# Attention and gated MLP on one core: a planned, pinned instruction order, fp32r transposes and column halves

## The chip, the core and the metric

The kernel runs on one core of a Trainium2 chip. The time is device microseconds of one execution; three runs of the kernel before gave a median of 826.99 us (826.61 to 827.62). A core has five instruction queues: TensorE (PE; its weight loads are shown apart as PEld), VectorE (DVE), ScalarE (ACT), GpSimd (POOL) and SyncE (SP), which here issues all DMA copies. Each queue is worked off in its order; an instruction that waits holds up those behind it.

## The reference

Attention over 8 batches of 8 heads, 576 tokens, head width 64, and then a gated MLP over each batch.

```
scores = q @ k.T / 8                       # per head, 576 x 576
cum    = cumsum(max(s, 0))                 # per head
scores = where(causal, -1e9, scores + min(-(cum[:, None] - cum[None, :]), 0))
attn   = softmax(scores)
x      = concat_heads(attn @ v)            # 576 x 512 per batch
h      = gelu_tanh(x @ w_in)               # 512 -> 1024
u, v   = h[:, :512], h[:, 512:]
v_n    = (v - mean(v)) / sqrt(var(v) + 1e-6) * g_ln
v_s    = w_sg @ v_n + b_sg[:, None]        # 576 x 576 over the tokens
out    = x + (u * v_s) @ w_out             # 512 -> 512
```

All inputs and the output are fp32 (the two weight matrices come as bits of 64-bit floats and are narrowed in the kernel).

## The kernel before

**Precision.** TensorE's fast type for 4-byte numbers here is fp32r. A product in fp32 quality is made of three fp32r products: each operand is split into a high part (a cast) and a low part (source minus high part), and high x high, high x low and low x high are added up in PSUM. `split` (L86) makes the two parts with one instruction on one engine and one on another. The first `NQ` = 8 heads do their scores, and the first `NP` = 12 heads their value products, in plain fp32 instead (tiles kf, qf, vf), which takes two instructions for each product and no splits.

**A head.** `load` (L102) fetches k, q and v; `split_head` (L272) splits them and copies rows into the combined operands by five DMA copies (L281 to L285). `scores` (L341) forms the causal 576 x 576 scores in five row blocks, of 448, 64, 320, 192 and 576 columns (the last in two halves), in two PSUM banks (ps_sc). `ttr` (L300) adds the mask and takes the row minimum on DVE (L305), `exp_` (L311) does the exponential with its row sum on ACT (L315), `norm` (L318) divides by the row sums on POOL (L338; ACT for one block of the fp32 heads). `transposes` (L365) turns the 13 blocks of 128 x 128 probabilities on TensorE (L377, in fp32, against an identity) into two banks (ps_pt) in four groups of 4, 4, 2 and 3; each group is evacuated by `evac` (ACT casts the high part, DVE subtracts the low one). `pv` (L432) multiplies them with v into the single bank xx (L450, L463 to L472), and ACT and DVE (L478, L479) add the upper and the lower 64 rows into the result tile xr, of which there are 8, four to a batch.

**A batch's MLP.** `ffn` (L484) splits xr into four xs tiles (POOL) and then does units of 12 to 14 matmuls: five v units (L518; the fifth, of 64 tokens, needs the last rows of xs side by side, which four DMA copies to xq bring, L528), eight u units (L582), eight s units (L597, L600, L601, the token mixing; L600 and L601 read the fifth v unit's result vnr), and eight o units (L616). Three banks (ps_m) serve these, in the last batch all but xx. After the v units DVE, ACT and POOL do the layer norm, and after each u unit the GELU.

**Order.** The text of the program is laid out on a time axis counted in heads: `place` puts steps at times (`POS`, L55), `spread` gives the units of a batch's MLP the stretch from 8b + 10 on, so that it lies beside the heads of the next batch. The framework's own scheduler (`schedule_with_timeline_sim=True`, L719) then moves instructions by its model of their durations. Weight blocks are fetched and split in the first 14 heads (`part`, L202); their DMA copies stand in `with later()` (L99), which puts them behind head 0's copy of cf (the cumulative sums) into k.

Of the kernel before, what the change touches and what calls it, by code (L numbers as in the profile page):

```python
# [40 lines left out]
         "o00 o01 s10 s11 s12 s13 o03 o02 o11 o13 o10 o12")  # L41
ORD0 = ("v0 v1 v2 v3 v4 u00 u01 u02 u10 u11 s00 u12 u03 s01 s03 u13 s02 o00 o01 s10 s11 s12 s13 o03 o02 o11 o13 o10 o12")
ORDL = ("v0 u00 v1 v2 u01 u02 v3 v4 u10 u11 s00 u12 u03 s01 s03 u13 s10 "
        "s02 o00 o01 s11 s12 s13 o03 o02 o11 o13 o10 o12")
CV = 1.4
# [5 lines left out]
MT = 52.0  # L51
F6 = [2.0, 9.4]
F7 = [2.0, 9.4]
F0 = [1.9, 9.6]
POS = dict(load=-1.8, split=-0.18, sc=(0, 0, 0, 0), tr=(0, 0, 0, 0), pv=(0, 0.1, 0.1), wv=(0.1, 6.0),  # L55
           wu=(7.0, 10.0), ws=(9.0, 11.0), wo=(11.0, 14.0), f0=2.0, f1=9.6)
# [3 lines left out]
def tile_attn_gmlp(  # L60
# [12 lines left out]
    nc = tc.nc  # L73

    const = ctx.enter_context(tc.tile_pool(name="const", bufs=1))
    att = ctx.enter_context(tc.tile_pool(name="att", bufs=2))
    moe = ctx.enter_context(tc.tile_pool(name="moe", bufs=1))
    ps_sc = ctx.enter_context(tc.tile_pool(name="ps_sc", bufs=2, space=bass.MemoryType.PSUM))
    ps_pt = ctx.enter_context(tc.tile_pool(name="ps_pt", bufs=2, space=bass.MemoryType.PSUM))
    ps_x = ctx.enter_context(tc.tile_pool(name="ps_x", bufs=1, space=bass.MemoryType.PSUM))  # L80
    ps_m = ctx.enter_context(tc.tile_pool(name="ps_m", bufs=3, space=bass.MemoryType.PSUM))
# [15 lines left out]
    first = []  # L97

    def later():  # L99
        return tc.issue_after(first[0].ins)  # L100

    def load(h):  # L102
        d = heads[h] = {}
        if h < NQ:
# [4 lines left out]
            x = nc.sync.dma_start(out=k[D:D + 1, :], in_=cf[h:h + 1, :])  # L109
            if h == 0:  # L110
                first.append(x)
        else:
            d["raw"] = att.tile([P, S], F32, name="raw", tag="raw", bufs=1)
            with later():
                nc.sync.dma_start(out=d["raw"], in_=kq[h, 0:2 * D])
# [3 lines left out]
        else:  # L119
            d["vr"] = att.tile([P, 6, D], F32, name="vr", tag="vr", bufs=1)  # L120
            with later():
                nc.sync.dma_start(out=d["vr"], in_=vp[h])

# [27 lines left out]
    load(0)  # L151
# [5 lines left out]
    ident = const.tile([P, P], F32, name="ident")  # L157
    nc.vector.memset(ident, 0.0)
# [14 lines left out]


    q2 = []
    pbuf = []
    sums = []
    for i in range(2):
        t = const.tile([66, S], F32R, name=f"q2_{i}")
# [3 lines left out]
        for it in range(5):  # L183
            t = const.tile([P, PW[it]], F32, name=f"p_{i}_{it}")
            if PW[it] > ITW[it]:
                nc.gpsimd.memset(t[:, ITW[it]:PW[it]], 0.0)
# [538 lines left out]
```

## Time and profile before

| | |
|---|---|
| median of three runs | 826.99 us |
| the profiled execution, its span | 828.8 us |
| PE busy | 792.6 us, 96% |
| DVE, ACT, POOL busy | 597.9, 576.5, 595.1 us, 70 to 72% |
| DMA | 89.29 MB, mean 108 GB/s |
| TensorE's clock, mean | 0.991 |

The span runs from the first instruction's start to the last one's end. Busy time is the union of an engine's instructions; matmuls overlap in a pipeline, so a matmul's duration in the trace is longer than the distance to the next one, and a busy TensorE may still be stalled. "Idle before, releaser" at the end of a row tells how long the engine did nothing before it, and what ended that. The chain of waits follows the last instruction back to what released it, step by step.

### The profile page before, as it was taken

Reading aid. Unit: us, or ns where it says so; the run is one execution under the profiler, and the core shown is the slowest. Engines: PE = TensorE matmul, PEld = TensorE weight load, DVE = VectorE, ACT = ScalarE, POOL = GpSimd, SP = SyncE. Lnnn points to the kernel's source line nnn. Section 1 sums busy time; section 2 is a strip of 40 time slices with the busy share of each in tenths; the row PEclk is TensorE's granted clock in tenths of the full one; section 3 lists DMA queues with packets and bytes.
Section 4 is the critical chain, followed back from the end, with each engine's and each line's share of the span. In section 5 each row is a group of like instructions: output and inputs, shape, how many; then the busy total and the mean of one; then the engine's idle time right before and its main releaser. Section 6 shows DMA issues by size and latency. Waiting matters only on the chain.

```text
span 828.8 us, 16733 instructions
## 1 busy us (share of the span) xinstructions
PE 792.6 (96%) x5161; PEld 696.1 (84%) x5161; DVE 597.9 (72%) x1806; ACT 576.5 (70%) x1620; POOL 595.1 (72%) x979
## 2 busy tenths in 40 slices
PE   6899999899999999999989999999999999999878
PEld 3355666889989998999979998899989998899778
DVE  5995468975787578966888577965888678963652
ACT  4787778775686678866878577866787677862430
POOL 4987668878677768796768778785778778872451
PEclk9999999999999999999999999999999999999989
DMA  7656553343442543444434453443444353400101
GB/s 210 215 158 181 148 139 84 86 105 100 116 106 74 128 125 86 108 121 126 112 82 104 115 139 90 113 109 96 119 119 103 100 152 93 98 26 23 35 8 57
DMA packets 69804, 89.29 MB, mean 108 GB/s; under 512 B 25954, under 2 KB 42212, under 8 KB 69716
## 3 DMA queue, kind: packets, MB, share of 16 engines
q1 hardware_dynamic: 69716, 88.23, 40.8%
q8 instruction: 41, 0.67, 0.4%
q14 instruction: 47, 0.39, 0.2%
HBM read 42.27 MB, written 9.73 MB: 63 GB/s over the span
## 4 chain that ended last, share of the span: by engine, by line
PE 73%; DVE 12%; DMA 5%; ACT 3%; issue 3%; POOL 2%; SPq 1%; DVEq 0%; POOLq 0%; ACTq 0%
PE om L616 12%; PE sm L597 11%; PE um L582 10%; PE xx L450 10%; PE vm L518 9%; PE pt L377 8%; PE sc L297 4%; PE sc L298 4%; DVE p L305 2%; DMA xq<-xs 2%; DMA q<-k 2%; PE sm L601 1%; PE sm L600 1%; DVE wbits L220 1%; DVE vm L504 1%
## 5 line engine op out<-in xcount | busy, mean ns | idle before, releaser
L338 POOL TENSOR_SCALAR p<-p,rs 128x448 f32<-128x448 f32 (+4 forms) x372 | 180.5, 499 | 29.1 <-DVE rs L321 9.6
L315 ACT ACTIVATE p<-p,mn 128x448 f32<-128x448 f32 (+4 forms) x320 | 177.9, 557 | 24.5 <-DVE mn L305 22.4
L305 DVE CUSTOM_DVE_ANT_0 p<-sc,mask 64x64 f32<-64x64 f32 (+4 forms) x320 | 126.2, 422 | 56.4 <-PE pt L377 31.0
L377 PE MATMUL pt<-ident,p 128*128 128x128 f32 (+1 forms) x832 | 137.2, 278 | 5.3 <-DVE pbl L389 2.6
L597 PE MATMUL sm<-ws,vn 128*128 128x288 f32 x768 | 130.3, 304 | 0.7 <-POOL vn L567 0.6
L93 POOL TENSOR_TENSOR k<-raw,k 128x576 fp32r<-128x576 f32 x56 | 80.3, 1433 | 66.7 <-ACT k L88 33.3
L582 PE MATMUL um<-xs,wi 128*128 128x288 f32 x768 | 123.4, 300 | 2.5 <-DVE u L504 2.4
L616 PE MATMUL om<-gt,wo 128*128 128x288 f32 x768 | 125.7, 298 | 0.0
L582 PEld LDWEIGHTS um<-xs,wi 128*128 128x128 f32 x768 | 108.9, 188 | 8.9 <-DVE u L504 4.0
L597 PEld LDWEIGHTS sm<-ws,vn 128*128 128x128 f32 x768 | 112.4, 192 | 3.3 <-DVE u L504 1.0
L377 PEld LDWEIGHTS pt<-ident,p 128*128 128x128 f32 (+1 forms) x832 | 96.8, 138 | 21.8 <-DVE pbl L389 5.4
L616 PEld LDWEIGHTS om<-gt,wo 128*128 128x128 f32 x768 | 110.6, 188 | 2.3
L518 PE MATMUL vm<-wi,xs 128*128 128x512 f32 x384 | 103.4, 399 | 0.0
L297 PE MATMUL sc<-k,q 128*128 128x448 f32 x336 | 100.8, 308 | 1.5 <-DVE mn L305 0.8
L298 PE MATMUL sc<-k,q 66*128 66x448 f32 x336 | 89.3, 298 | 0.6 <-DMA k<-cum 0.6
L88 ACT CAST pbh<-pt 128x512 fp32r<-128x512 f32 x104 | 48.9, 479 | 58.8 <-PE pt L377 58.8
L518 PEld LDWEIGHTS vm<-wi,xs 128*128 128x128 f32 x384 | 69.7, 189 | 14.9 <-POOL xs L93 1.6
L93 POOL TENSOR_TENSOR gt<-u,gt 128x288 fp32r<-128x288 f32 x64 | 50.7, 806 | 41.6 <-ACT gt L88 41.1
L297 PEld LDWEIGHTS sc<-k,q 128*128 128x128 f32 x336 | 60.8, 181 | 9.1 <-DVE mn L305 3.9
L93 DVE TENSOR_TENSOR pbl<-pt,pbh 128x512 fp32r<-128x512 f32 x104 | 56.5, 549 | 15.9 <-ACT pbh L88 15.9
L298 PEld LDWEIGHTS sc<-k,q 66*128 66x128 f32 x336 | 60.9, 181 | 5.9 <-issue 0.9
L88 ACT CAST k<-raw 128x576 fp32r<-128x576 f32 x56 | 37.6, 671 | 39.5 <-PE sc L297 33.8
(142 smaller groups left out, 1704.8 us busy)
## 6 DMA issues: line engine op xcount, KB each, us to landing
q<-k SPq DMA_DIRECT2D x168, 144.0 KB
raw<-in_kq SPq DMA_DIRECT2D x56, 288.0 KB
vr<-in_vp SPq DMA_DIRECT2D x52, 192.0 KB
out_t<-ot SPq DMA_DIRECT2D x64, 144.0 KB
k<-k SPq DMA_DIRECT2D x56, 144.0 KB
wraw<-in_w_in SPq DMA_DIRECT2D x16, 256.0 KB
kf<-in_kq SPq DMA_DIRECT2D x8, 288.0 KB
qf<-in_kq SPq DMA_DIRECT2D x8, 288.0 KB
```

Of the source, the lines that this page charges most:

```text
L88: nc.scalar.copy(out=hi, in_=src)
L93: eng_lo.tensor_tensor(out=lo, in0=src, in1=hi.bitcast(F32), op=ALU.subtract)
L297: nc.tensor.matmul(o, d["q1"][:, i0:i0 + r], d["k1"][:, j0:j1], start=True, stop=False)
L298: nc.tensor.matmul(o, q2[h % 2][:, i0:i0 + r], d["k2"][0:66, j0:j1], start=False, stop=True)
L305: nc.vector.tensor_tensor_reduce(out=pbuf[h % 2][it][0:r, j0:j1], in0=pst[0:r, c0:c0 + j1 - j0], in1=(mask2 if it in (2, 4) else mask)[0:r ...
L315: nc.scalar.activation(out=p, in_=p, func=AF.Exp, bias=d["mn"][0:r, it:it + 1], scale=-1.0, accum_out=sums[h % 2][0:r, it:it + 1])
L338: e.tensor_scalar(out=po, in0=pi, scalar1=f, scalar2=1.0, op0=ALU.mult, op1=ALU.mult)
L377: nc.tensor.transpose(out=ps[0:n, c:c + P], in_=pb[it][:, jb:jb + n], identity=ident)
L518: nc.tensor.matmul(ps[0:r], xs[c][:, xi, ts_], wi[:, c, wj, fs], start=(n == 0), stop=(n == 11))
L582: nc.tensor.matmul(ps[:, 0:CH], wi[:, c, wj, dt * P:(dt + 1) * P], xs[c][:, xi, cs], start=(n == 0), stop=(n == 11))
L597: nc.tensor.matmul(ps[:, 0:CH], vn[j][:, vi, ds_], ws[:, j, wj, cs], start=(n == 0), stop=False)
L616: nc.tensor.matmul(ps[:, 0:CH], wo[:, c, wj, ms], gt[ch, c][:, gi, :], start=(n == 0), stop=(n == 11))
```

## The change

1. **A planner writes the order.** Every engine call is recorded as an `Op` with its dependencies (by tile slot and region) and a cost (`cost`). `Plan.order` walks through them as a list scheduler: for each engine the earliest-written operation that is ready is taken; an operation becomes ready when its inputs' ends plus a latency for its engine (`LAT`, 454 ns for PE) have passed. Matmuls in a `group()` stay together; others may be interleaved one by one. The program is then issued in this order and not moved again (`manual_schedule`). SBUF slots are laid out by hand (`Ring`), and a slot can be held until `drop`. In its profile every engine instruction bears line 211, that of `issue`; its tiles tell them apart.
2. **Transposes in fp32r**: the probabilities are read through a second name of the same memory (`rbuf`) and the identity and the output are fp32r.
3. **14 result tiles** xr instead of 8; the xs splits are placed apart from the MLP units, earlier on the axis (`xsplit`).
4. **Column halves in fp32 heads**: the value products alternate between rows 0 to 63 and 64 to 127 of the xx bank; a third ACT copy and a DVE addition bring both together.
5. The `later()` around weight copies is gone; a head's k and v loads and splits are placed separately; four o units move ahead of three s units in each batch.

The counts of instructions are the same on TensorE, POOL and SP; DVE and ACT have 12 more each.

```diff
-ORDER = ("v0 u00 v1 u01 v2 u02 v3 v4 u10 u11 s00 u12 u03 s01 s03 u13 s02 "
-         "o00 o01 s10 s11 s12 s13 o03 o02 o11 o13 o10 o12")
+ORDER = ("v0 u00 v1 u01 v2 u02 v3 v4 u10 u11 s00 u12 u03 s01 s03 u13 s02 "
+         "o00 o01 s10 o03 o02 s11 s12 s13 o11 o13 o10 o12")
...
-POS = dict(load=-1.8, split=-0.18, sc=(0, 0, 0, 0), tr=(0, 0, 0, 0), pv=(0, 0.1, 0.1), wv=(0.1, 6.0),
-           wu=(7.0, 10.0), ws=(9.0, 11.0), wo=(11.0, 14.0), f0=2.0, f1=9.6)
+POS = dict(lk=-1.9, lkf=-1.55, lv=-1.35, lvf=-0.45, sk=-1.1, sv=-0.4, sc=(0, 0.15, 0.3, 0.4), cx=(1.0, 1.1, 1.2, 1.25, 1.35, 1.4, 1.45, 1.5), wv=(0.1, 6.0), wu=(5.0, 9.0),
+           ws=(8.5, 11.0), wo=(10.5, 13.0), f0=10.0, x0=2.4)
+LAT = dict(PE=454.0, ACT=136.0, DVE=136.0, POOL=185.0, SP=160.0)
+XR = 14
...
+    def order(self, lat=LAT):
...
+        while True:
+            best = None
+            for e, r in ready.items():
+                if r:
+                    t = max(free[e], min(r)[0])
+                    if best is None or t < best[0]:
+                        best = t, e
+            if best is None:
+                break
+            t, e = best
+            r = ready[e]
+            k = min(k for x, k in r if x <= t)
+            r.remove((rt[k], k))
+            o = ops[k]
...
+            for u in o.users:
+                q = ops[u]
+                q.left -= 1
+                if q.eng == e and e != "SP" and k not in q.raw:
+                    x = free[e]
+                else:
+                    x = end[k] + lat[q.eng]
+                rt[u] = max(rt[u], x)
+                if not q.left:
+                    push(u)
...
+    def issue(self, order):
+        for k in order:
+            for fn, args, kw in self.ops[k].calls:
+                fn(*args, **kw)
...
+    pbuf = [[pools[f"p{it}"]([P, PW[it]], F32, "p", i) for it in range(5)] for i in range(2)]
+    rbuf = [[pools[f"p{it}"]([P, PW[it]], F32R, "r", i) for it in range(5)] for i in range(2)]
...
-            nc.tensor.transpose(out=ps[0:n, c:c + P], in_=pb[it][:, jb:jb + n], identity=ident)
+            nc.tensor.transpose(out=ps[0:n, o:o + P].bitcast(F32R), in_=pb[it][:, jb:jb + n], identity=ident)
...
+        def mm(o0, o1, jt, m, side=0, k=P, **kw):
+            o = xx[D * side:D * side + rows, o0:o1]
+            nc.tensor.matmul(o, st(jt)[0:k], m, **{"start": False, "stop": False, **kw})
...
+        if f32:
+            with nc.group():
+                mm(64, 512, 1, pb_[0][:, 320:768], side=1, start=True)
+                mm(0, 512, 0, pa[0], start=True)
...
         if f32:
...
+            with nc.group():
+                mm(128, 448, 2, pb_[0][:, 0:320], side=1)
+                mm(192, 384, 3, pd[0][:, 128:320])
+                mm(0, 64, 0, pd[0][:, 64:128], side=1, stop=True)
+                mm(256, 320, 4, pd[0][0:REM, 0:64], k=REM, stop=True)
+            with nc.group():
+                nc.scalar.copy(out=xt[hs, 0:64], in_=xx[64:128, 0:64])
+                nc.scalar.copy(out=xt[hs, 64:128], in_=xx[0:64, 0:64])
+                nc.scalar.copy(out=xt[hs, 128:S], in_=xx[64:128, 64:512])
+            nc.vector.tensor_tensor(out=xt[hs, 128:S], in0=xx[0:64, 64:512], in1=xt[hs, 128:S], op=ALU.add)
...
+    def xsplit(b, c):
+        t = moe.tile([P, 2, S], F32R, name="xs", tag="xs", bufs=4)
+        split(t[:, 0, :], t[:, 1, :], xr[(b, c)], *eng("xs"))
+        xsb.setdefault(b, []).append(t)
...
+    order = nc.order()
+    if PROBE is not None:
+        PROBE.append(nc)
+    with tc.manual_schedule():
+        nc.issue(order)
```

**Three places in the order.** In the names of the change, tiles are called after their slots: u is the slot that xq takes, gt the one of the weight blocks (wraw) and of the gated products, xs the one of cf, psx the bank xx, psp the transposes' banks, psm the MLP's and pss the scores' banks.

The first copies on SP, before:

```order
L128 DMA st<-in_s_t 128x320
L107 DMA kf<-in_kq 128x576
L108 DMA qf<-in_kq 128x576
L118 DMA vf<-in_vp 128x6x64
L107 DMA kf<-in_kq 128x576
L108 DMA qf<-in_kq 128x576
L118 DMA vf<-in_vp 128x6x64
L109 DMA kf<-cf 1x16x36 x2
L212 DMA wraw<-in_w_in 128x512 x2
```

and now (the rows up to the second vf are as above, with one weight block among them):

```order
L211 DMA gt_52_121<-in_w_in 128x512
L211 DMA gt_63_132<-in_w_in 128x512
L211 DMA gt_68_137<-in_w_in 128x512
L211 DMA gt_77_146<-in_w_in 128x512
L211 DMA raw_118_187<-in_kq 128x576
L211 DMA g_b_32_101<-in_g_ln 128x512
L211 DMA vr_196_265<-in_vp 128x384
L211 DMA k1_24_93<-xs_23_92 1x16x36
L211 DMA k1_43_112<-xs_23_92 1x16x36
```

Five weight blocks, raw, g_b and vr have moved ahead of the two cf rows (k1 from xs).

The xq copies of the fourth batch on SP, before:

```order
L283 DMA q_6031<-k_6030 64x576
L284 DMA k_6029<-k_6029 64x576
L528 DMA xq<-xs 128x2x64
L122 DMA vr<-in_vp 128x384
L285 DMA k_6030<-cum 2x576
L528 DMA xq<-xs 128x2x64 x3
L281 DMA q_6209<-k_6207 64x576
```

and now:

```order
L211 DMA k_701_770<-k_701_770 64x576
L211 DMA u_765_834<-xs_727 128x2x64
L211 DMA k_702_771<-cum 2x576
L211 DMA out_t<-u_704_773 128x288
L211 DMA vr_768<-in_vp 128x384
L211 DMA u_765_834<-xs_737 128x2x64
L211 DMA u_766_835<-xs_745 128x2x64
L211 DMA u_766_835<-xs_750 128x2x64
L211 DMA q_724_793<-k_722_791 64x576
```

All four (u from xs) stand ahead of the next head's copies (q_724). On TensorE that head's scores and transposes now come before the matmuls that read them:

```order
L211 MATMUL pss1_59<-k1_722_791,q1_724_793 128x288
L211 MATMUL pss1_59<-k2_723_792,q2_0_33_102 128x288
L211 MATMUL psp1_61<-ident_28_97,r_18_84 128x128
L211 MATMUL psp1_61<-ident_28_97,r_17_83 128x128
L211 MATMUL psp1_61<-ident_28_97,r_16_82 128x128
L211 MATMUL psp1_61<-ident_28_97,r_19_85 128x128
L211 MATMUL psp0_60<-ident_28_97,r_18_84 128x128 x2
L211 MATMUL psp0_60<-ident_28_97,r_17_83 128x128
L211 MATMUL psp0_60<-ident_28_97,r_19_85 128x128
L211 MATMUL psm0_63<-xs_658_727,wi_37_106 128x288 x2
L211 MATMUL psm2_65<-wi_37_106,u2_765_834 128x512
```

Eight transposes stand in a row, in both banks, where before a group of four stood alone.

The value products of an fp32 head on TensorE, before:

```order
L450 MATMUL xx<-pbh,vf 64x448
L450 MATMUL xx<-pbh,vf 64x320
L518 MATMUL vm<-wi,xs 128x512 x3
L295 MATMUL sc<-kf,qf 128x288
L518 MATMUL vm<-wi,xs 128x512 x3
L295 MATMUL sc<-kf,qf 128x288
L450 MATMUL xx<-pdh,vf 64x192
L468 MATMUL xx<-pdh,vf 64x64
L469 MATMUL x_420<-pdh,vf 64x64
```

and now:

```order
L211 MATMUL psm_64<-wi_106,xs_208 128x512
L211 MATMUL psx_62<-pbh_148,vs_131 64x448
L211 MATMUL psx_62<-pah_144,vs_131 64x512
L211 MATMUL psx_62<-pbh_148,vs_131 64x320
L211 MATMUL psx_62<-pdh_149,vs_131 64x192
L211 MATMUL psx_62<-pdh_149,vs_131 64x64 x2
```

All six products of the head (a 512 column one among them, which stood earlier before) now stand together, in alternating column halves.

More of the change, by code (lines that the diff above doesn't have):

```diff
@@ L72, in tile_attn_gmlp @@
 ):
[L73 to L81, printed above, removed]
+    nc0 = tc.nc
@@ L95, in tile_attn_gmlp, with load_k @@
     heads = {}
[L97 to L103, printed above, removed]
+    def load_k(h):
+        d = heads.setdefault(h, {})
         if h < NQ:
@@ L175, in tile_attn_gmlp @@
     q2 = []
-    pbuf = []
     sums = []
@@ new lines, in evac, with st @@
+        def evac(ts, c0, ps, w, e=nc.scalar):
+            if f32:
+                (e.copy if e is nc.scalar else e.tensor_copy)(out=ts[0][:, c0:c0 + w], in_=ps[:, 0:w])
+            else:
+                hi, lo = (t[:, c0:c0 + w] for t in ts)
+                split(hi, lo, ps[:, 0:w], nc.scalar, nc.vector)
+        def st(jt):
+            return d["v"][:, jt, :] if f32 else d["vs"][:, jt, :, :].rearrange("p a d -> p (a d)")
+        t = bank()
+        with nc.group():
+            for o, it in ((128, 3), (384, 2), (0, 1), (256, 4)):
+                tr(t, o, it, 0)
@@ new lines, in context @@
+        pa = new("pa", 512)
+        evac(pa, 0, t, 512)
+        yield
+        t = bank()
+        with nc.group():
+            tr(t, 384, 3, 128)
+            tr(t, 0, 3, 256)
+            tr(t, 256, 2, 256)
+            tr(t, 128, 4, 256)
+        pb_ = new("pb", 768)
+        evac(pb_, 0, t, 512, nc.vector)
+        yield
+        xx = ps_x.tile([P, 512], F32, name="xx", tag="xx")
+        def mm(o0, o1, jt, m, side=0, k=P, **kw):
+            o = xx[D * side:D * side + rows, o0:o1]
+            nc.tensor.matmul(o, st(jt)[0:k], m, **{"start": False, "stop": False, **kw})
@@ new lines, in context @@
+        if not f32:
+            mm(0, 512, 0, pa[0], start=True)
+        yield
+        t = bank()
+        with nc.group():
+            tr(t, 128, 2, 128)
+            tr(t, 0, 4, 128)
+        evac(pb_, 512, t, 256)
+        if not f32:
+            mm(0, 512, 0, pa[1])
+        yield
+        t = bank()
+        with nc.group():
+            tr(t, 0, 4, 512, 64)
+            tr(t, 64, 3, 384)
+            tr(t, 192, 4, 384)
+        if f32:
+            pd = [att.tile([P, 320], F32, name="pdh", tag="pdh", bufs=1)]
+            nc.vector.tensor_copy(out=pd[0][0:64, 0:64], in_=t[0:64, 0:64])
+            nc.vector.tensor_copy(out=pd[0][:, 64:320], in_=t[:, 64:320])
+        else:
+            hi, lo = pd = [att.tile([P, w], F32R, name="pd" + x, tag="pd" + x, bufs=1)
+                           for x, w in (("h", 320), ("l", 192))]
@@ L429, in transposes @@
             nc.vector.tensor_tensor(out=lo, in0=t[:, 128:320], in1=hi[:, 128:320].bitcast(F32), op=ALU.subtract)
-        yield 0.35
-    def pv(h):
-        d = heads[h]
-        pt = d["pt"]
-        f32 = h < NP
-        c, half = h % H // 2, h % 2
-        key = (h // H, c)
+        yield
+        if f32:
+            with nc.group():
+                mm(64, 512, 1, pb_[0][:, 320:768], side=1, start=True)
+                mm(0, 512, 0, pa[0], start=True)
+        else:
+            with nc.group():
+                for m in pb_:
+                    mm(128, 448, 2, m[:, 0:320])
+        yield
+        if not f32:
+            with nc.group():
+                for m in pb_:
+                    mm(64, 512, 1, m[:, 320:768])
+        yield
         if key not in xr:
```

525 lines of the change are left out of this document (366 added, 159 removed).

## The prediction

> **What bounds the kernel now.** I read the page first (busy times, clock), then a table of stretches, then the chain of waits, and last the timeline of TensorE for the distance between two starts.
>
> ```profile
> span 828.8 us, 16733 instructions
> PE 792.6 (96%) x5161; PEld 696.1 (84%) x5161; DVE 597.9 (72%) x1806; ACT 576.5 (70%) x1620; POOL 595.1 (72%) x979
> ...
> PEclk9999999999999999999999999999999999999989
> ...
> PE om L616 12%; PE sm L597 11%; PE um L582 10%; PE xx L450 10%; PE vm L518 9%; PE pt L377 8%; PE sc L297 4%; PE sc L298 4%; DVE p L305 2%; DMA xq<-xs 2%; DMA q<-k 2%; PE sm L601 1%; PE sm L600 1%; DVE wbits L220 1%; DVE vm L504 1%
> ```
> TensorE (PE) is busy nearly all the time, and the chain runs along it; no other engine is over 72%. But busy time counts a stalled pipeline as busy, so I also want the work. The stretches (length; busy us and instructions of PE, PEld, DVE, ACT, POOL; clock; DMA share; GB/s):
>
> ```profile
> 0.00:12.00 12.00, 6.11 (x18) 5.14 (x19) 5.08 (x14) 2.75 (x4) 5.22 (x15) 1.00 0.56 156
> 12.00:94.00 82.00, 74.07 (x316) 39.55 (x315) 62.49 (x205) 61.31 (x187) 65.28 (x92) 1.00 0.64 189
> ...
> 510.00:604.00 94.00, 92.17 (x640) 85.62 (x639) 71.64 (x221) 71.25 (x200) 71.73 (x119) 1.00 0.43 112
> ...
> 779.00:829.00 50.00, 40.47 (x273) 38.85 (x271) 22.87 (x49) 15.50 (x34) 19.55 (x39) 0.92 0.11 35
> ```
> There are four stages: the start (0 to 12), eight heads with fp32 scores while weights are prepared (12 to 94), steady batches, and the last batch's feed-forward part alone. In the second, DVE and POOL are near 78% beside a PE at 90%. The chain shows how long a steady batch is, since the same wait returns in each:
>
> ```profile
> 416.02 4.01 DMA xq<-xs
> 510.27 3.03 DMA xq<-xs
> 603.67 3.43 DMA xq<-xs
> ```
> The distances are 94.25 and 93.40, so 93.8 us for a batch. The work in it comes from other pieces of the chain, which hold the distances of whole groups, and for the transposes from a merged row of the timeline (start, length, name, count):
>
> ```profile
> 118.05 2.79 PE vm L518 x12
> ...
> 249.37 3.18 PE um L582 x24
> ```
>
> ```profile
> 400.57 0.60 PE L377 MATMUL pt<-ident,p 128*128 128x128 f32 x4
> ...
> L377 PE MATMUL pt<-ident,p 128*128 128x128 f32 (+1 forms) x832 | 137.2, 278 | 5.3 <-DVE pbl L389 2.6
> ```
> 2.79 / 12 = 0.2325 us for a matmul of 512 columns (L518), 3.18 / 24 = 0.1325 for one of 288 (L582, and likewise L597 and L616). Of the four transposes' 0.60 the last one's latency is 0.278; the other three start (0.60 - 0.278) / 3 = 0.107 apart. I count 0.109 with what follows the last. So a column costs (232.5 - 132.5) / 224 = 0.446 ns, and a matmul 4 ns more. Feed-forward: 304 x 0.1325 + 56 x 0.2325 = 53.3 us. A head: 12 score matmuls with 3200 columns and 10 value matmuls with 3072 columns are 2.9 us, the short ones among them 0.3 more (held up by their weight loads, below), and 13 transposes 1.4: 4.6, or 36.7 for eight. Together 90.0, which leaves 3.8 us of a batch's 93.8 lost. **TensorE's work bounds the kernel, and about 4% of a steady batch is lost to waits.**
>
> **The change, part by part.** *Transposes in fp32r.* 832 of them, now at 0.109. No fp32r transpose is in the trace. Its stream, by the column price, is 128 x 0.446 + 4 = 61 ns. Its weight load is bounded by ordinary fp32r loads behind short matmuls (weight loads, by their starts):
>
> ```profile
> 410.30 0.19 PEld L472 LDWEIGHTS x<-pdh,vs 128*128 128x128 f32 x1
> 410.44 0.19 PEld L450 LDWEIGHTS xx<-pdl,vs 128*128 128x128 f32 x1
> 410.55 0.19 PEld L450 LDWEIGHTS xx<-pdh,vs 128*128 128x128 f32 x1
> 410.68 0.42 PEld L377 LDWEIGHTS pt<-ident,p 128*128 128x128 f32 x4
> 411.07 0.30 PEld L582 LDWEIGHTS um<-xs,wi 128*128 128x128 f32 x2
> ```
> The first three start 0.14, 0.11 and 0.13 apart while the matmuls between them stream for 0.03 to 0.09, so such a load takes about 0.11. But the four loads of the fp32 transposes fit into 411.07 - 410.68 = 0.39, 0.098 each: a load for a transpose can be shorter. Ends: 61 and 109. I take the middle, 85: 832 x 24 ns = 20 us. In the twelve fp32 heads (156 transposes) PE isn't the only limit, so these count half: **-18**; at the ends 0 and -40.
>
> *Column halves in the fp32 heads' value products.* Now each of the six products is two instructions into 64 columns of the array, one after the other:
>
> ```profile
> 60.20 1.50 PE L450 MATMUL xx<-pbl,vf 128*64 128x448 f32 x4
> 61.63 1.24 PE L295 MATMUL sc<-kf,qf 128*128 128x288 f32 x4
> 62.80 0.54 PE L450 MATMUL xx<-pdh,vf 128*64 128x192 f32 x2
> 63.27 0.33 PE L468 MATMUL xx<-pdh,vf 64*64 64x64 f32 x2
> 63.52 0.33 PE L469 MATMUL x<-pdh,vf 128*64 128x64 f32 x2
> 63.78 0.66 PE L377 MATMUL pt<-ident,p 128*128 128x128 f32 x4
> ```
> The products of 448 and 320 columns take 61.63 - 60.20 = 1.43, hence 512 columns 0.95; the others 0.47, 0.25 and 0.26: 3.36 us a head. After the change they alternate between two column halves, 832 columns on one side and 768 on the other. If the halves overlap fully, a head takes 832/1600 of it, 1.75, and twelve heads save 19; if not at all, nothing. No row shows two halves at once. I take two thirds, **-13**, since the trailing product has no partner and PE isn't all that limits these heads.
>
> [...]
>
> The price is a DVE addition for each of these heads, 64x448, and one more small ACT copy:
>
> ```profile
> L479 DVE TENSOR_TENSOR xr<-xx,xr 64x512 f32<-64x512 f32 x52 | 35.4, 681 | 11.8 <-ACT xr L478 10.6
> ```
> 0.6 x 12 = 7 us of DVE. DVE has 19.5 us free of the 82 in the second stage; where its queue is full, the addition comes late and holds the one xx bank. Between 0 and 7: **+2**.
>
> *The order.* The four xq copies are what a steady batch waits for. Their issue stands behind others in SP's queue, and TensorE stands still:
>
> ```profile
> 415.71 0.26 SPq L285 DMA_DIRECT2D k<-cum  x1
> 416.02 3.27 SPq L528 DMA_DIRECT2D xq<-xs  x3
> ...
> 420.07 0.50 PE L532 MATMUL vm<-wi,xq 128*128 128x512 f32 x1 [1.82 <-DMA xq<-xs]
> ```
> In the new order all four stand in SP's queue ahead of the five copies of a later head, and TensorE reads them only after that head's score matmuls. They have therefore landed before the copies that those scores wait for. That wait goes; the 3.8 us won't go entirely, for the short matmuls' loads remain and other waits (for DVE, for scores) come up. I take 2.5 us a batch over (738 - 150) / 93.8 = 6.3 batches: **-16**, between 0 and -24. What is late next is the landing of the heads' own q and k copies, which the new order keeps behind xq.
>
> The last batch has the same wait and one for vnr:
>
> ```profile
> 781.81 0.47 PE L532 MATMUL vm<-wi,xq 128*128 128x512 f32 x1 [1.71 <-DMA xq<-xs]
> 796.75 0.80 PE L597 MATMUL sm<-ws,vn 128*128 128x288 f32 x4 [0.64 <-POOL vn L567]
> 801.18 1.30 PE L600 MATMUL sm<-wr,vnr 128*128 128x288 f32 x4 [3.63 <-DVE vnr L567]
> ```
> That is 6.0 us, and the last stretch above has a clock of 0.92 over 50 us, 4.0 more. The new order puts the fifth v unit earlier and 120 matmuls (16 us) between it and the first that reads vnr; before, 71 (9.4 us) stood there. I take **-6** of the 10.
>
> *The start.* Weight loads no longer wait for head 0's row of cf.
>
> ```profile
> 4.03 0.56 SPq L118 DMA_DIRECT2D vf<-in_vp  x1
> 8.97 1.24 SPq L109 DMA_DIRECT2D kf<-cf  x2
> ...
> 11.95 2.94 PE L295 MATMUL sc<-kf,qf 128*128 128x448 f32 x10
> ...
> GB/s 210 215 158 181 148 139 84 86 105 100 116 106 74 128 125 86 108 121 126 112 82 104 115 139 90 113 109 96 119 119 103 100 152 93 98 26 23 35 8 57
> ```
> Before, nothing is issued between 4.6 and 8.97, and the scores begin at 11.95. Now five weight blocks of 256 KB, a raw of 288, g_b of 256 and a vr of 192 (the page's sizes) are ahead of the two cf rows: 2016 KB more, 10 us at the 210 GB/s of the first slices. Part of it drains before 8.97, so the first scores come up to 8 us later. Against that, weight preparation starts earlier, work which holds DVE and POOL in the second stage anyway. Between 0 and +8: **+4**.
>
> The 14 result buffers and the moved xs splits stand behind the order's term; they add no instruction. Sum: -18 - 13 + 2 - 16 - 6 + 4 = -47. The profiled execution took 828.8; the median is 1.8 below that. 828.8 - 47 - 1.8 = **780 us**.
>
> **Rivals.** *A: the transposes stay bound by their loads* at 0.109, as the loads 0.11 apart say; against it the 0.098. Then 18 us stay: 798. [...]
>
> *B: the order gives nothing back.* The xq wait is replaced by others, since all engines stand at 70% and each queue is still in order. For it: the many small waits that remain around DVE p L305 (2% of the chain). Then 22 us stay: 802.
>
> *C: all of it is won*: transposes at 61 (22 more), full halves (6 more), 3.8 us a batch (8 more): 744. Against it, weight loads near 0.1 us.
>
> *D: slower.* The pinned order runs two banks of transposes, eight in a row, and the third group must reuse the first bank. That bank is free only after ACT's cast and DVE's subtraction.
>
> ```profile
> L93 DVE TENSOR_TENSOR pal<-pt,pah 128x512 fp32r<-128x512 f32 x52 | 35.6, 685 | 16.0 <-ACT pah L88 16.0
> ...
> L88 ACT CAST pah<-pt 128x512 fp32r<-128x512 f32 x52 | 30.5, 586 | 1.2
> ```
> Of these 0.59 and 0.68 us four transposes (0.36) cover little. TensorE's queue is in order, so everything behind it waits, and DVE's next subtraction comes late in turn. 0.91 us in each of 64 heads is 58 us: 838. Slower begins at 47 / 64 = 0.73 us a head. Against it: in the steady order value and feed-forward matmuls stand between the two groups in most heads; before, such waits are short because 6 to 12 matmuls (0.8 to 1.6 us) stand there.
>
> **How the numbers follow.** The forecast has 0.50, A 0.16, B 0.12, C 0.12, D 0.10. A and B together would be 820, still faster. The range for 8 in 10 takes in A and B whole and all but the end of C: 748 to 810. Differences under 0.2% (1.7 us) are what a measurement of this kernel can't tell from none. Faster: all but D and a little of D's mild end, 0.90; within 0.2%: 0.02, D at just its threshold; slower: 0.08.
>
> **What would show it.** After the change, transposes: starts 0.085 apart in runs of four or eight, against 0.109 in A and 0.061 in C. The fp32 value products: pairs whose starts are closer than a stream, about 1.75 to 2.3 us a head. A batch of 93.8 - 2.5 - 8 x 13 x 0.024 = 88.8 us; in B 91.3, with new releasers before PE. First scores between 12 and 20 us. D would show as idle TensorE before a transpose with ACT or DVE as releaser. I would be wrong altogether if DVE or POOL reached 90% in the second stage, or if the clock fell below 1.00 in more slices than before.

## The result, and the profile after

The changed kernel takes 806.73 us (median of 4 runs, 804.88 to 809.74), the kernel before, beside it, 826.8: a ratio of 0.9759, 95% interval 0.9737 to 0.9782. That is 20 us faster, less than half of the 47 forecast. The profiled execution, the slowest of the four, has a span of 808.0 us, 20.8 below the 828.8 of before.

The page of the changed kernel (span, busy time of TensorE, granted clock, chain by engine):

```profile
span 808.0 us, 16764 instructions
PE 767.8 (95%) x5161; PEld 684.8 (85%) x5161; DVE 614.5 (76%) x1818; ACT 579.4 (72%) x1632; POOL 598.6 (74%) x979
...
PEclk9899989999998999999999999999999999999999
...
PE 65%; DVE 13%; ACT 9%; POOL 4%; issue 4%; DMA 3%; SPq 1%; ACTq 0%; POOLq 0%; DVEq 0%
```
TensorE's busy time fell by 25 us, close to the span's 21; its share of the chain fell from 73% to 65%. The clock row has three slices at 8 in the first third, where before had none.

To see where the time went I cut both spans at the first read of xq in the batches 0, 2 and 6, so that each piece holds nearly the same work: the start with the fp32 heads, two batches, four steady batches, and the rest. Stretches of before, then of the changed kernel (length; busy us and instructions of PE, PEld, DVE, ACT, POOL; clock; DMA share; GB/s):

```profile
0.00:122.30 122.30, 107.69 (x476) 62.46 (x476) 84.11 (x279) 86.37 (x252) 87.89 (x138) 1.00 0.62 174
122.30:324.30 202.00, 196.71 (x1327) 178.28 (x1326) 152.10 (x457) 146.43 (x414) 156.47 (x257) 0.99 0.41 105
324.30:700.50 376.20, 370.22 (x2561) 344.28 (x2560) 287.77 (x881) 284.60 (x801) 287.94 (x473) 1.00 0.44 110
700.50:828.80 128.30, 117.94 (x803) 111.10 (x802) 73.92 (x192) 59.13 (x156) 62.85 (x114) 0.97 0.15 41
```

```profile
0.00:123.50 123.50, 98.05 (x484) 63.96 (x484) 97.12 (x300) 92.11 (x270) 98.33 (x149) 0.93 0.59 170
123.50:320.80 197.30, 192.48 (x1342) 178.49 (x1341) 151.66 (x462) 148.65 (x420) 150.27 (x246) 0.98 0.42 110
320.80:691.80 371.00, 365.71 (x2563) 337.36 (x2562) 294.15 (x883) 282.92 (x801) 287.50 (x473) 1.00 0.42 112
691.80:808.00 116.20, 111.61 (x778) 104.94 (x777) 71.58 (x178) 55.68 (x143) 62.49 (x114) 1.00 0.15 44
```
The pieces differ by +1.2, -4.7, -5.2 and -12.1. The largest gain is in the last piece, but not all of it is gain: 25 of its matmuls (803 before, 778 now) stand ahead of the cut in the changed kernel, and the first two pieces hold 8 and 15 more. At 0.13 us for each that is some 3 us. The four steady batches hold the same work (2561 and 2563) and give 1.3 us each (92.75 against 94.05), where 5.0 was forecast. In the first piece TensorE works 9.6 us less and nothing is gained. The changed kernel's first scores start at 15.38, before at 11.95.

### The profile page after: what moved, and what is told of

Its sections match the earlier page's. It is cut to its first block, busy times and chain, and to the rows that moved or that the text cites. A ratio compares the mean times of both kernels' runs of the same rounds, so it can differ in the third digit from the quotient of the medians.

```text
span 808.0 us, 16764 instructions
## 1 busy us (share of the span) xinstructions
PE 767.8 (95%) x5161; PEld 684.8 (85%) x5161; DVE 614.5 (76%) x1818; ACT 579.4 (72%) x1632; POOL 598.6 (74%) x979
## 4 chain that ended last, share of the span: by engine, by line
PE 65%; DVE 13%; ACT 9%; POOL 4%; issue 4%; DMA 3%; SPq 1%; ACTq 0%; POOLq 0%; DVEq 0%
PE psm L211 39%; PE pss L211 10%; PE psx L211 9%; PE psp L211 7%; ACT p L211 3%; DVE p L211 3%; DVE u L211 3%; ACT vt L211 2%; DVE vt L211 2%; DMA raw<-in_kq 2%; POOL k L211 1%; DVE bs L211 1%; DVE xr L211 1%; POOL p L211 1%; ACT pbh L211 1%
## 5 line engine op out<-in xcount | busy, mean ns | idle before, releaser
L211 ACT ACTIVATE p<-p,mn 128x192 f32<-128x192 f32 (+4 forms) x320 | 178.7, 559 | 76.6 <-DVE mn L211 66.1
L211 PE MATMUL pss<-k,q 128*128 128x288 f32 (+9 forms) x768 | 157.8, 321 | 11.6 <-DVE mn L211 7.7
L211 PEld LDWEIGHTS pss<-k,q 128*128 128x128 f32 (+3 forms) x768 | 121.1, 184 | 40.3 <-DVE mn L211 17.1
L211 DVE CUSTOM_DVE_ANT_0 p<-pss,mask 128x192 f32<-128x192 f32 (+4 forms) x320 | 126.9, 421 | 29.6 <-PE pss L211 27.1
L211 PE MATMUL psm<-xs,wi 128*128 128x288 f32 x708 | 117.3, 301 | 2.5 <-DVE u L211 1.6
L211 PE MATMUL psm<-gt,wo 128*128 128x288 f32 x720 | 118.7, 300 | 0.0
L211 PE MATMUL psm<-wi,xs 128*128 128x512 f32 (+1 forms) x392 | 118.4, 404 | 0.0
L211 PE MATMUL psm<-ws,vn 128*128 128x288 f32 x708 | 115.7, 301 | 0.0
L211 PEld LDWEIGHTS psm<-gt,wo 128*128 128x128 f32 x720 | 103.0, 189 | 0.8
L211 PEld LDWEIGHTS psm<-ws,vn 128*128 128x128 f32 x708 | 102.2, 191 | 1.7 <-DVE u L211 1.0
L211 PEld LDWEIGHTS psm<-wi,xs 128*128 128x128 f32 (+1 forms) x392 | 67.1, 184 | 10.3 <-issue 0.8
L211 ACT CAST pbh<-psp 128x512 fp32r<-128x512 f32 x104 | 49.5, 476 | 11.6 <-PE psp L211 11.4
```

The lines of the kernel that those rows point to most:

```text
L211: fn(*args, **kw)
```

## The experiments

In the order of the questions. A difference of two ratios is uncertain by about 0.0035, or 3 us. Two theories stood at the start: *stage* (TensorE's savings count only where TensorE sets the time) and *order* (they count everywhere, and the new order itself costs what is missing). One thing limits most of these runs: an edit that adds or takes away an operation lets the planner draw a new order. By the traces DVE's instructions stand in the same order where only the transposes' type, the filling or the width of the statistics differs, and in another order in every other run.

**1. What each part is worth.** The transposes back in fp32:

```diff
-    ident = const.tile([P, P], F32R, name="ident")
+    ident = const.tile([P, P], F32, name="ident")
...
-        pb = rbuf[h % 2]
+        pb = pbuf[h % 2]
...
-            nc.tensor.transpose(out=ps[0:n, o:o + P].bitcast(F32R), in_=pb[it][:, jb:jb + n], identity=ident)
+            nc.tensor.transpose(out=ps[0:n, o:o + P], in_=pb[it][:, jb:jb + n], identity=ident)
```


> The changed kernel with its transposes back in fp32 (same order of the instructions, same column halves). In the changed kernel the fp32r transposes start 0.085 us apart, before they started 0.109 apart. Stage theory (TensorE sets the time only in part; in the first 120 us and in the stretches where DVE is full its savings are idle time): 52 heads x 13 x 0.016 = 11 us come back, 816 to 820. Order theory (every saving of TensorE counts, and the new order itself costs what is missing): 832 x 0.024 = 18 to 20 us come back, 825 to 827.

Measured: 815.3 us, ratio 0.9844 (0.9811 to 0.9877). 7 us come back, less than either theory said.

Without the column halves:

```diff
-                mm(64, 512, 1, pb_[0][:, 320:768], side=1, start=True)
                 mm(0, 512, 0, pa[0], start=True)
+                mm(64, 512, 1, pb_[0][:, 320:768])
...
+            x0 = bank()
...
-                mm(0, 64, 0, pd[0][:, 64:128], side=1, stop=True)
+                nc.tensor.matmul(x0[0:D, 0:64], st(0), pd[0][:, 64:128], start=True, stop=True)
...
-            nc.vector.tensor_tensor(out=xt[hs, 128:S], in0=xx[0:64, 64:512], in1=xt[hs, 128:S], op=ALU.add)
+            nc.scalar.copy(out=xt[hs, 64:S], in_=xx[0:D, 0:512])
...
```


> The changed kernel with the fp32 heads' value products as before: one after the other in one half of the columns, the first block in a bank of its own, no DVE addition. The halves save 1.1 us of TensorE in each of twelve heads. Stage theory: at most 2 us come back (within 806 to 809), because DVE and POOL, at 86 and 87% between 12 and 94 us, set these heads. Order theory: 12 x 1.1 = 13 come back, 820.

Measured: 811.7 us, 0.9800 (0.9769 to 0.9830): 3.4 us come back, more than the stage theory's 2 and far from the order theory's 13.

Both edits together:

> The changed kernel with fp32 transposes and without the column halves: only the new order, its 14 result banks and its earlier weight copies are left of the change. Stage theory: 817 to 822, so the order alone is still 5 to 10 us faster than the kernel before (the last batch's gain of 12, less what a batch loses). Order theory: 806.7 + 13 + 19 = 838 to 840, slower than before by 12.

Measured: 819.5 us, 0.9890 (0.9861 to 0.9918): the order alone is 9 us faster than the kernel before, 7 to 11. The order theory falls. Put in one after the other, order, transposes and halves are worth 0.0110, 0.0090 and 0.0041, which must add up to the whole change's 0.0241. With the halves put in ahead of the transposes, the two are worth 0.0046 and 0.0085: nearly the same, so neither needs the other. By the same pieces the order alone is:

```profile
0.00:126.70 126.70, 109.05 (x484) 66.63 (x485) 91.78 (x289) 89.09 (x260) 98.04 (x149) 0.99 0.57 165
126.70:324.10 197.40, 194.70 (x1342) 179.70 (x1342) 152.04 (x460) 148.70 (x419) 149.63 (x246) 1.00 0.42 110
324.10:700.90 376.80, 371.11 (x2561) 344.69 (x2561) 294.99 (x881) 282.84 (x801) 287.15 (x473) 1.00 0.42 110
700.90:818.50 117.60, 112.73 (x779) 106.03 (x777) 72.16 (x178) 55.70 (x143) 62.38 (x114) 1.00 0.15 43
```
Against before: +4.4 in the first piece, -4.6, +0.6 in the four steady batches, -10.7 in the last piece (with 8 and 15 matmuls more in the first two, and 24 fewer in the last). So the order gains nothing in the four steady batches. The transposes do: the two pairs that differ in them alone are 5.7 us apart there with the halves (376.7 and 371.0) and 4.1 without (376.8 and 372.7).

**2. Where the order's steady gain went.** What TensorE waited for in the four steady batches, of before and of the order alone (total us, times, longest):

```profile
PE vm L532 <- DMA xq<-xs: 2.9, 3, 1.8
PE um L582 <- DVE u L504: 1.1, 4, 0.3
PE sm L601 <- DMA vnr<-vnr: 1.1, 2, 0.6
```

```profile
PE pss L211 <- DVE mn L211: 2.2, 8, 0.3
PE psm L211 <- DMA vnr<-vnr: 1.1, 2, 0.6
PE psm L211 <- DVE u L211: 0.8, 4, 0.2
```
The xq wait was worth 2.9 us in four batches, 0.7 each, and not 2.5. It is gone, and 2.2 us of short waits for the minimum (mn) have come in its place; TensorE's whole idle time is 6.0 us before and 5.7 in the order alone. That is rival B, in the steady batches. A run that moves those copies alone:

```diff
+            if tt == NT - 1:
+                for c2 in range(2):
+                    t = moe.tile([P, 2, 2, REM], F32R, name="xq", tag="u2", bufs=U2)
+                    for i in range(2):
+                        nc.sync.dma_start(out=t[:, i].bitcast(F32), in_=xs[2 * c2 + i][:, :, NT * P:S].bitcast(F32))
...
             else:
-                xq = []
-                for c2 in range(2):
...
```


> The kernel before with the four xq copies of a batch issued at the start of the fourth v unit in place of the fifth, two or three places earlier in SP's queue and ahead of the next head's copies in most batches; nothing else. The prediction gave this wait 2.5 us in each of 6.3 steady batches and 1.7 in the last: 17 us, 810 to 814. The trace of before, asked by tile, has TensorE waiting for xq 4.6 us in four of eight batches: 0 to 5 us faster, 822 to 827.

Measured: 844.6 us, 1.0221 (1.0192 to 1.0250), 18 us slower: a miss for both. What TensorE waits for at the tile xq, before and in this run (total us, times):

```profile
  DMA xq<-xs: 4.6, 4
```

```profile
  DMA xq<-xs: 1.7, 1
```
The wait went as meant, but the program before is put in order by simulated times, and instructions on all engines changed place with the edit. So the 18 us can't be laid on the copies. What the run does show is that a kernel can lose this wait and get slower.

**3. Whether DVE paces the steady batch.** The layer norm's statistics over 64 of 512 columns only (the result is then another):

```diff
-            nc.vector.bn_stats(out=bs[0:r], in_=ps[0:r])
+            nc.vector.bn_stats(out=bs[0:r], in_=ps[0:r, 0:64])
```


> The changed kernel with the statistics of the feed-forward part taken over 64 of 512 columns (the results are then not the reference's; the order is the same): 0.4 to 0.5 us of DVE less in each of 40 units, 2 to 2.5 us in a batch, all of it in the stretch where DVE is over 85% busy. If DVE paces that stretch: a batch 2 to 2.5 us shorter, 788 to 793. If TensorE's pipeline sets the batch: under 0.6 us a batch, 802 to 807.

Measured: 807.2 us, 0.9771 (0.9743 to 0.9799): no gain. Its four steady batches:

```profile
319.70:692.00 372.30, 365.05 (x2563) 338.57 (x2562) 282.83 (x881) 282.21 (x801) 288.33 (x473) 1.00 0.42 112
```
DVE works 11 us less there than in the changed kernel (282.8 against 294.2), and the batches are no shorter. DVE doesn't pace them; TensorE, 98.6% busy, does.

**4. Whether the half clock eats the savings.** A piece of the first stage of the changed kernel, as stretches:

```profile
24.30:27.70 3.40, 1.29 (x5) 0.38 (x4) 3.25 (x15) 3.40 (x13) 3.22 (x6) 1.00 0.49 136
27.70:34.60 6.90, 6.65 (x23) 4.09 (x25) 3.41 (x12) 3.76 (x12) 6.71 (x11) 0.51 0.40 141
```
TensorE is idle for part of 3.4 us, and the next 6.9 run at half clock. There are five such pieces in the span, 24 us of half clock, four of them in the first 117 us. The kernel before has 14 us, half of it in the last batch, and the order alone one piece of 3.4. A run that fills the idle time:

```diff
+            n, dst = self.fill.get(k, (0, None))
+            for _ in range(n):
+                self.nc.tensor.matmul(dst[:, 0:P], self.ident, self.ident, start=True, stop=True)
...
+        if h < 10:
+            nc.fill[len(nc.ops)] = 14, ps_m.t[0] if h < 4 else t
```


> The changed kernel with idle-time matmuls that compute nothing needed: 50 of 128 columns ahead of the first scores and 14 ahead of the first transpose group of each of heads 0 to 9, into a bank that is free there; same order otherwise. In the changed kernel's profile TensorE ran at half its clock for 24 us in five pieces of 3.4 or 6.8 us, each after a 3.4-us stretch in which it was less than 75% busy; in the run with the order alone it was 5.5 us. Clock theory (the halves and the faster transposes turn TensorE's work into idle time, and the idle time into half clock): half clock falls below 10 us and the end comes 4 to 9 us earlier, 798 to 803. Stage theory (DVE and POOL set the first 120 us): the clock stays up, the end moves by less than 2 us, 805 to 809.

```profile
PEclk9999999999999999999999999999999999999999
```
The clock stays up (0.98 from 12 to 94 us, where the changed kernel has 0.94), and the time is 807.9 us, 0.9778 (0.9752 to 0.9804): nothing gained. Since the 190 added matmuls take TensorE's time too, this shows the net of both, and not what the clock alone is worth.

**5. What holds the fp32 heads.** Without one of DVE's three narrowing operations on the weights, then with the filling too:

```diff
-        nc.vector.scalar_tensor_tensor(out=w, in0=l32, scalar=29, in1=w,
-                                       op0=ALU.logical_shift_right, op1=ALU.bitwise_or)
```


> The changed kernel without the third of the DVE operations that narrow a weight block (the lowest three mantissa bits of the weights are left out, so the results differ a little): some 13 us of DVE's work less, nearly all between 12 and 150 us. If DVE sets the fp32 heads: 4 to 10 us faster, 797 to 803. If TensorE's work or its clock does, or POOL: 0 to 2 us, 805 to 807.

> The changed kernel without the third narrowing operation and with the idle-time matmuls that keep TensorE's clock up in the first ten heads. The run without that operation had 27 us of half clock in its profile at 802. If the clock counts once DVE has room: 3 to 6 us faster than that, 796 to 799. If it doesn't, as beside a full DVE: 801 to 804.

Measured: 801.8 us, 0.9699 (0.9675 to 0.9724), 5 us faster than the changed kernel; with the filling 809.5, 0.9772 (0.9736 to 0.9807), a miss for both values forecast. So where DVE has room, the filling costs 6 us net, and the clock's part is not to be had in this way. Without the addition that joins the halves:

```diff
-            nc.vector.tensor_tensor(out=xt[hs, 128:S], in0=xx[0:64, 64:512], in1=xt[hs, 128:S], op=ALU.add)
```


> The changed kernel without the DVE addition that joins the two column halves in the twelve fp32 heads (one half of those heads' value products is then missing from the result): 12 x 0.6 = 7 us of DVE less, TensorE's work as in the changed kernel; the planner may shift a few places. If DVE's volume sets the fp32 heads, as the run without the third narrowing operation says (13 us of DVE less there gave 5 us): 2 to 4 us faster, 803 to 805. If the price of the addition is its place (the single product bank is held until it is done, and TensorE waits for it): 5 to 9 us faster, 798 to 802. If it costs nothing: 806 to 808.

Measured: 809.2 us, 0.9776 (0.9748 to 0.9803). By the pages DVE works 6 us less here (608.4 against 614.5) and nothing is gained; without the narrowing operation it works 15 less (599.3) and 5 us are gained. That speaks for the kind of DVE work and against its sum, but weakly: in proportion the 6 would have given 2 us, less than the uncertainty. The weights at the places of the kernel before (wu too, on the line above, from (5.0, 9.0) to (7.0, 10.0)):

```diff
...
-           ws=(8.5, 11.0), wo=(10.5, 13.0), f0=10.0, x0=2.4)
+           ws=(9.0, 11.0), wo=(11.0, 14.0), f0=10.0, x0=2.4)
```


> The changed kernel with the weight blocks at the places of the kernel before (the u half from head 7 to 10 in place of 5 to 9, the gate's from 9, the output's from 11 to 14): DVE's and POOL's narrowing work moves some 10 to 20 us later, none of it goes. If DVE's sum over the first 150 us decides: no change, 805 to 808. If it is the crowding between 30 and 90 us: 2 to 5 us faster, 802 to 805.

Measured: 809.0 us, 0.9783 (0.9762 to 0.9804): no gain, so the early weights are not what costs. Then all three narrowing operations left out, and on top of that two of POOL's normalizations on DVE:

```diff
-        nc.vector.tensor_scalar(out=w, in0=w, scalar1=3, scalar2=0x3FFFFFFF, ...)
-        nc.vector.scalar_tensor_tensor(out=w, in0=h32, scalar=-0x40000000, in1=w, ...)
-        nc.vector.scalar_tensor_tensor(out=w, in0=l32, scalar=29, in1=w, ...)
```


> The changed kernel without all three DVE operations that narrow a weight block (the weights are then wrong, and so is the result; ACT's, POOL's and the DMAs' work on them stays): 24 x 3 x 0.55 = 40 us of DVE less, nearly all before 150 us. If DVE's narrowing ahead of the heads' own operations sets the first 120 us: the fp32 heads run at TensorE's pace, 12 to 22 us faster, 785 to 795. If POOL or the chain through a head sets them: no more than the 5 us that one operation of the three gave, or little beyond it, 798 to 803.

```diff
...
-'n0': 'gggsg'
+'n0': 'ggvsv'
...
```


> The run without DVE's three narrowing operations (weights and result wrong), with the normalization of two of the five score blocks (576 and 320 columns) of the twelve fp32 heads moved from POOL to DVE: some 14 us of POOL less, as much DVE more. If POOL took DVE's place as the limit of these heads: 4 to 10 us faster than 800, 790 to 796. If not (ACT, or the chain through a head whatever the load): 797 to 802.

Measured: 800.1 us, 0.9651 (0.9625 to 0.9677), and 798.9 us, 0.9655 (0.9636 to 0.9675). The first piece of the former:

```profile
0.00:111.90 111.90, 89.80 (x472) 61.43 (x473) 62.51 (x227) 88.44 (x265) 87.05 (x146) 0.94 0.66 187
```
DVE is down to 56% there, and the piece is 11.6 us shorter; by the ratios the gain is 9 us. No engine is over 80% of the piece any more (TensorE 80, ACT 79, POOL 78). Moving some of POOL's work to DVE adds nothing. And the halves in these three settings:

> The changed kernel without the third narrowing operation of the weights (lowest three mantissa bits left out) and without the column halves. Against the run without that operation alone (802) it tells what the halves are worth where DVE has room. If DVE is what kept their 13 us of TensorE from counting: 7 to 12 us more, 809 to 814. If they are worth the same 3 to 4 us as beside a full DVE, the limit is another (POOL, the chain through a head): 804 to 807.

> The same without the column halves. If DVE's narrowing is what kept the halves' TensorE time from counting, the distance to the run with them is 8 to 13 us; if it is 2 to 4 us as in the two pairs measured so far, TensorE's time in the value products is off the path of these heads for another reason.

> The same without the column halves. If the other engines' load is what keeps the halves from counting, the distance to the run with them grows from 5 to 8 to 13 us. If it stays at 3 to 6, a head's chain of stages, not an engine's load, hides the rest.

Measured: 804.3, 805.6 and 802.5 us; 0.9723 (0.9703 to 0.9744), 0.9714 (0.9688 to 0.9740) and 0.9700 (0.9684 to 0.9715). With the two pairs above, the halves are worth 0.0041, 0.0046, 0.0024, 0.0063 and 0.0045: 2 to 5 us, 3.6 in the mean, whatever room DVE or POOL has. Each pair also differs in its order, so a single one says little; the five together say it.

The halves alone in the kernel before:

```diff
+        if f32:
+            yield 0.2
+            mm(64, 512, 1, pb[0][:, 320:768], side=1, start=True)
+            mm(0, 512, 0, m[0], start=True)
...
+            nc.vector.tensor_tensor(out=xt[hs, 128:S], in0=xx[0:64, 64:512], in1=xt[hs, 128:S], op=ALU.add)
```


> The kernel before, in its own order, with the column halves alone in the fp32 heads' value products (and the DVE addition that they need). TensorE is 90% busy there between 12 and 94 us, DVE 76%. If TensorE's work counts in this stage as the kernel before ran it, 12 x 1.1 us = 10 to 13 us faster (814 to 817). If the stage goes by DVE, POOL and the chains through them, 0 to 2 us (825 to 827).

Measured: 834.6 us, 1.0074 (1.0040 to 1.0108), 6 us slower: a miss for both. The stretch 12 to 94, and the chain by engine:

```profile
12.00:94.00 82.00, 67.82 (x315) 38.49 (x314) 61.45 (x209) 63.19 (x194) 69.32 (x92) 0.96 0.66 189
...
PE 69%; DVE 9%; DMA 7%; POOL 7%; ACT 4%; issue 2%; SPq 1%; POOLq 0%; DVEq 0%; ACTq 0%
```
TensorE works 6.2 us less than before in that stretch, POOL 4.0 more, and POOL's share of the chain goes from 2% to 7%. This program, too, was put in order anew, so that the loss can't be laid on POOL: cut as above, its first piece is 2.7 us longer than before's (125.0 against 122.3), and the two batches behind it 4.8 (206.8 against 202.0).

**6. One number of the planner.** It counts an arrival at TensorE with 454 ns:

```diff
-LAT = dict(PE=454.0, ACT=136.0, DVE=136.0, POOL=185.0, SP=160.0)
+LAT = dict(PE=136.0, ACT=136.0, DVE=136.0, POOL=185.0, SP=160.0)
```


> The changed kernel planned with 136 ns for an arrival at TensorE in place of 454, so without the delayed arrivals: the same instructions in an order that lets TensorE take its next group closer behind what it waits for. If the small waits of TensorE for DVE in the steady batch are what the order costs, they grow: 0.5 to 1.5 us a batch, 810 to 816. If the order's places don't decide: 804 to 809.

> The changed kernel planned with 800 ns for an arrival at TensorE in place of 454. With 136 the whole gain was lost (829). If more distance between a producer and TensorE still helps: 802 to 805. If 454 is about the best place: 806 to 812.

Measured: 829.3 us, 1.0003 (0.9971 to 1.0036) with 136, and 829.5, 1.0014 (0.9996 to 1.0031) with 800. Both are a miss for every value forecast, and both lose the whole gain, though the transposes and the halves are still in. (With 136 the ten executions lie between 820.8 and 841.6, so the median is loose, but the fastest, too, is 14 us behind the changed kernel.) With 800, TensorE's waits and the stretch for the four steady batches are:

```profile
PE psp L211 <- POOL p L211: 5.0, 8, 0.8
PE pss L211 <- DVE mn L211: 3.8, 8, 0.7
PE psm L211 <- DVE u L211: 3.1, 8, 0.6
PE psm L211 <- DVE vnr L211: 2.6, 4, 0.7
```

```profile
322.10:704.50 382.40, 367.75 (x2563) 338.04 (x2562) 290.52 (x881) 280.60 (x801) 286.95 (x473) 1.00 0.41 109
```
The waits are 14.5 us there, against 2.2 for mn and less than 1 each for the rest in the changed kernel, and the batches are 11.4 us longer. If the transposes and the halves are worth their 11 us there too, which no run shows, an order that brings 9 us at 454 costs as much at either side of it.

Of those that compute the whole result, the run without the third narrowing operation is the fastest, 5 us below the changed kernel, at the price of the weights' lowest three bits.

## Why the prediction was wrong, by its steps

**The bound and the lost 3.8 us.** That TensorE's work bounds the steady batches holds (98.6% busy, and DVE's relief is worth nothing). The step that failed is the next one, that the 3.8 us left of a batch's 93.8 are waits, of which 2.5 can be had. The 3.8 were a remainder of a sum of estimates. By the stretches of before TensorE was idle 6.0 us in four batches, 1.5 each, and waited for xq 0.7 of it. The chain's rows of 4.01, 3.03 and 3.43 tell how long the copy was on the chain, not how long TensorE stood still; the one quoted wait of 1.82 was the longest of three. Asked by engine, the waits would have shown it. The order's term of -16 is -4.0 in the profile (-4.6 and +0.6), or -6 if the 15 matmuls more in the second piece are counted at 0.13 us each, and all of it lies in the first two batches.

**Transposes.** Forecast -18, measured -7 (two pairs with the same order, 0.0085 and 0.0090). The spacing was right (0.085 forecast, 0.080 in a run of eight), the sum was not. A run of eight and a run of three in the order alone, with the instruction behind, and the same places in the changed kernel (start, length):

```profile
524.39 1.04 PE L211 MATMUL psp<-ident,p 128*128 128x128 f32 x8
525.18 0.64 PE L211 MATMUL psm<-xs,wi 128*128 128x288 f32 x3
...
528.45 0.49 PE L211 MATMUL psp<-ident,p 128*64 128x128 f32 x3
528.70 0.39 PE L211 MATMUL psx<-pbh,vs 128*128 128x320 f32 x1
```

```profile
518.09 0.80 PE L211 MATMUL psp<-ident,r 128*128 128x128 f32 x8
518.73 0.63 PE L211 MATMUL psm<-xs,wi 128*128 128x288 f32 x3
...
521.96 0.37 PE L211 MATMUL psp<-ident,r 128*64 128x128 f32 x3
522.17 0.38 PE L211 MATMUL psx<-pbh,vs 128*128 128x320 f32 x1
```
With a last latency of 0.28 (the mean length of such a transpose), eight in fp32 are (1.04 - 0.28) / 7 = 0.109 apart; in fp32r, with 0.24, (0.80 - 0.24) / 7 = 0.080. Rival A is out: it had 0.109 for the fp32r transposes. But the next instruction starts 0.79 and 0.64 after the first of eight, so 0.03 behind the last in fp32 and 0.08 in fp32r. The prediction counted "0.109 with what follows the last": a run of eight cost 0.79 and not 0.87, one of three 0.25 and not 0.33. The eight save 0.15, the three 0.04, where 24 ns each would be 0.19 and 0.07. Per steady batch this gave 1.0 and 1.4 us in the two pairs (4.1 and 5.7 over four) in place of 2.5, 10 to 14 ns a transpose. In the first piece, with the fp32 heads, nothing is gained by it (127.6 us against 126.7 with fp32, and 123.5 against 120.8). Why the instruction behind starts later stays open.

**Halves.** The mechanism came out at its best end. A head in the changed kernel:

```profile
50.67 0.59 PE L211 MATMUL psx<-pbh,vs 128*64 128x448 f32 x1
50.67 0.64 PE L211 MATMUL psx<-pah,vs 128*64 128x512 f32 x1
51.09 0.54 PE L211 MATMUL psx<-pbh,vs 128*64 128x448 f32 x1
51.15 0.59 PE L211 MATMUL psx<-pah,vs 128*64 128x512 f32 x1
...
51.75 0.80 PE L211 MATMUL psx<-pdh,vs 128*64 128x192 f32 x5
52.47 1.24 PE L211 MATMUL pss<-k,q 128*128 128x288 f32 x4
```
Two products start together and run together. A head's products take 52.47 - 50.67 = 1.80 us in place of 3.36, as full overlap says (1.75). Twelve such heads at full clock would free 19 us of TensorE, and the time falls by 3.6. The failed step is the weight that I gave to it: the two thirds should have been a fifth. The addition's +2 was 0, within the 3 us of a difference. What limits these heads is narrowed down, not settled: no run shows the addition, or the two of POOL's five normalizations that were moved, to be it; DVE's narrowing is part of it (9 us for all of it), and with it gone the halves are still worth only 5 us. Part of what they save on TensorE goes to the clock. With them its busy time in the first piece is 10.3 and 12.7 us lower (98.1 against 108.4, 96.4 against 109.1) and not 19, and from the clocks of the stretches 12 to 94 and 94 to 150 (length times what is missing to 1.00) it loses 3 to 7 us more to half clock than without them in four of the five pairs (0.94 and 0.94 in the changed kernel, 0.96 and 0.97 without the halves); in the fifth the clock of the whole execution is 0.991 against 0.996. Whether the time would be shorter at full clock stays open, since the filling has a price of its own. Between 12 and 94 us TensorE waits, by the list of the changed kernel, most ahead of the transposes (psp); the 3.6 us are the wait at the start:

```profile
PE psp L211 <- POOL p L211: 6.8, 7, 2.2
...
PE pss L211 <- DMA cum<-xs: 3.6, 1, 3.6
...
PE pss L211 <- DVE mn L211: 2.9, 5, 1.8
...
PE psp L211 <- ACT pah L211: 2.3, 2, 1.6
```
That fits a head's own chain (scores, minimum, exponential, normalization, transposes), in which the products aren't a link, but no run has shortened that chain or relieved ACT.

**Start and tail.** The start's +4 was right: 3.4 us by the first scores, 4.4 by the first piece of the order alone, which holds 8 matmuls more. The changed kernel's first scores:

```profile
15.38 1.83 PE L211 MATMUL pss<-k,q 128*128 128x448 f32 x2 [3.57 <-DMA cum<-xs]
```
By the timeline of SP the copies of the two cf rows are issued at 10.57, before at 8.97, and the scores start 4.8 us after that in place of 3.0. So 1.6 us are the later issue and 1.8 a longer way from there, which fits copies that stand behind the weights' copies. The releaser named (cum) is a copy that these scores don't read.

The tail's -6 was near. The last piece is 10.7 us shorter by the order, of which 24 matmuls that moved ahead of the cut make 3.2 at 0.1325 us each. That leaves 7.5 of the 10 listed: TensorE's idle time falls from 10.4 to 4.9, and its clock goes from 0.97 to 1.00. The transposes bring 1.4 more.

**The sum.** Order -9 for -18, transposes -7 for -18, halves with their price -3.6 for -11. Each of the three terms is about half or less of its forecast. The time is near rival B's 802, but came another way: half of what the order was to give came, most of it in the tail, and the other two parts gave less than half. DVE or POOL at 90%, or a lower clock in more slices, were named as what would make the prediction wrong: DVE and POOL reached 86 and 87% between 12 and 94 us, and the clock did fall, to 0.94 there.

```profile
12.00:94.00 82.00, 65.68 (x318) 41.02 (x318) 70.66 (x218) 65.25 (x199) 71.24 (x96) 0.94 0.60 178
```

## What to carry to other kernels

Before a wait is priced, list all waits of the bound engine in that stage by releaser and tile: a row of the chain gives the length of a link, and only the list gives the idle time that can be won. Price a faster instruction by the distance from the first of its run to the instruction behind the last, since a gain inside the run can be paid back there (here 0.029 us won at each of seven steps, 0.05 lost behind the eighth). A saving on an engine that stands at 90% beside others at 78% counted for a fifth here. A list schedule's parameters can move the time by as much as the change itself, so a part's worth should be measured under one fixed order; of the parts here only the transposes' was.

## What the runs showed of the hardware that I had not expected

- Half clock came without a long idle time: TensorE was busy 1.29 of 3.40 us, its longest idle time there was 1.84, and the next 6.9 us were granted at 0.51, as shown above. Nor does the length of the idle time decide alone: in the same execution 3.57 us of it ahead of the first scores were followed by full clock (1.00 from 15.38 to 27.50).
- In the runs of eight shown above, what stood behind the last fp32 transpose started 0.03 us after it, behind the last fp32r transpose 0.08, though the fp32r ones followed each other faster (0.080 against 0.109).
- Two fp32 products with 64 output rows each, in different column halves, overlapped wholly in the head shown above, both passes of each: starts 50.67 and 50.67, then 51.09 and 51.15.
